# A convolution and MLP kernel on one core: first groups of 6, 8, 10 and 16 tokens, the fourth in the seven-product form, and fewer scaling steps in the last group

## The chip, the cores and the metric

The kernel runs on one core of one Trainium2 chip. The metric is device time in microseconds. The kernel before took 977.64 us (median of three runs, 976.54 to 978.36). A core has a matrix engine (PE, with weight loads shown apart as PEld), VectorE (DVE), ScalarE (ACT), GpSimd (POOL) and SyncE (SP), each with a queue of its own that it works through in program order, and 16 DMA engines.

## The reference

The input x is 8 sequences of 4224 tokens with 192 features, float32. A causal convolution of 7 taps runs along the tokens; the taps are a softmax over `weight` and each of 8 heads (24 features) has its own. On its result y follows an MLP with layer norm and a residual:

```python
mu = np.mean(x, axis=-1, keepdims=True)
var = np.mean((x - mu) ** 2, axis=-1, keepdims=True)
xn = (x - mu) / np.sqrt(var + 1e-06) * g_ln
ch = np.maximum(xn @ w_ch1, 0.0) @ w_ch2
return (x + ch).astype(np.float32)
```

Here x is y, w_ch1 is 192 x 768 and w_ch2 is 768 x 192.

## The kernel before

**Tiling.** Each of 128 partitions holds consecutive tokens; a group is n tokens on every partition. `groups` (L70) lists 18: group 0 (6 tokens), group 1 (8, the tokens left over at the ends of the sequences), group 2 (11), group 3 (15), and 14 groups of 16 (groups 4 to 17). Groups 0, 2 and 3 together are the first sequence.

**Steps of a group g.**
- `load_x` (L132) brings x with 6 tokens of halo to the tile `xg`. `first_tap` (L376, ACT or DVE) and `conv` (L408, DVE, one instruction for each tap and head) make y. In some groups `second_tap` (L393) makes the second tap on ACT and adds it to y by a DMA that accumulates (L403).
- `transpose` (L419, DVE) makes yt, with 32 features by token as PE wants it. `moments` (L431, DVE) takes statistics; `root` (L443) turns those of two groups into reciprocal standard deviations by 18 small POOL operations. The mean and g_ln are folded into w1 at the start; the reciprocal deviation is applied behind the MLP.
- `store_y` (L475) writes y to the output. The MLP's part is scaled by ACT (`scale`, L831) and added to the output in DRAM by accumulating DMAs on POOL's queue (`add_to_out`, L835). The last group is added on DVE and stored by SP.

**Up and down.** The first matmul ("up", to 768 hidden features) exists in two forms. `up` (L538) runs 144 float32 matmuls of n x 32 columns, all at L532, evicted from PSUM by ACT with the relu. `up_mixed` (L591) cuts tokens, features and two thirds of the hidden features in halves and forms seven products of sums in place of eight, with sums of w1 (`sums_of_quarters`, L562, made once) and of yt (`sums_of_y`, L575); partial results are added by accumulating DMAs (`close`, L615); the last third is plain. That is 216 matmuls, 168 of them with 256 columns and 48 with 512. The second matmul ("down") is plain in `down` (L671, 144 matmuls at L685) or in `down_fast` (L719), seven products of 36 matmuls at L738. `half_sum` and `lower_sum` (L700, L707) make its left operands on DVE, `finish_fast` (L801) its output.

Which form a group takes before the change:

| groups | up | down |
|---|---|---|
| 0, 1, 2 | plain | plain |
| 3 | plain | seven products |
| 4 to 16 (`MIXED`, L81) | seven products | seven products |
| 17 (last) | plain, 11 and 5 tokens apart | seven products on 11 tokens, plain on 5 |

**Order.** It is written out by hand: the loop at L896 and the functions issue the work of group g on PE together with DVE's, ACT's and the queues' work for groups g+1 and g+2. Inside `up_mixed(g)` stand the taps of group g+1 and the scaling of group g-1; inside `down_fast(g)` the first two taps of group g+2 between the products (`taps_behind`, L761), the transpose of g+1 and its first ten moments. Buffers of x, y and statistics exist twice, all others once; the eight PSUM banks are taken in turn, four at a time by up and one at a time by down.

Around groups 2 and 3 this order is special: iteration 2 issues both taps of group 4, the load of group 5 and the store of group 3 on POOL's queue (L914 to L918); behind `down` come `moments(3)`, `root(2)` for groups 2 and 3, and `finish(2)`, which transposes group 2's output from the copies that `park` (L812) made piece by piece. Iteration 3 stores group 4 and loads group 6 on POOL's queue (L942 to L946) and makes the sums of w1 inside `down_fast(3)` (L780). From iteration 4 on, load and store go to SP and each two iterations are alike.

Of the kernel before, what the change touches and what calls it, by code (L numbers as in the profile page):

```python
# [7 lines left out]
F32 = mybir.dt.float32  # L8
# [8 lines left out]
def kernel(  # L17
# [29 lines left out]
    nc = tc.nc  # L47
    PSUM = bass.MemoryType.PSUM
    B, S, D = x.shape
    H, K = weight.shape  # L50
    F = moe_w_ch1.shape[1]
    P = 128
# [4 lines left out]
    J = 16  # L57
    R = 2 * J
    LEFT = (S - P * R) * B // P
# [7 lines left out]

    groups = [(0, 0, 6), (None, 0, LEFT), (0, 6, J - 5), (0, J + 1, J - 1)]  # L70
    groups += [(b, j0, J) for b in range(1, B) for j0 in (0, J)]
    assert PAD <= 6 and max(n for _, _, n in groups) <= J
    NG = len(groups)
# [4 lines left out]
    NFAST = max(fast.values())  # L78
    T = C // 2

    MIXED = range(4, NG - 1)  # L81
    PAIR = NF // 2 - 1
    HJ = J // 2
    EARLY = 10
# [323 lines left out]
    def conv(g, k0=1, k1=K, heads=(0, H)):  # L408
        n = groups[g][2]
        t = xg[g]  # L410
        for k in range(k0, k1):
            for h in range(*heads):
                cs = slice(h * GRP, h * GRP + GRP)
                nc.vector.scalar_tensor_tensor(  # L414
                    out=y[g][:, 0:n, cs], in0=t[:, k : k + n, cs], scalar=taps[:, h, k : k + 1],
                    in1=y[g][:, 0:n, cs], op0=ALU.mult, op1=ALU.add,
                )
# [10 lines left out]

    sums = {}

    def moments(g, j1=0, j2=None):  # L431

        n = groups[g][2]
        if j1:
            pass
        elif g % 2:
            sums[g] = sums[g - 1][:, groups[g - 1][2] :]
        else:
            sums[g] = spool.tile([P, 2 * J, nc.vector.BN_STATS_DIM], F32, tag="st", name=f"st{g}")
        for j in range(j1, n if j2 is None else j2):  # L440
            nc.vector.bn_stats(out=sums[g][:, j, :], in_=y[g][:, j, :])  # L441

    def root(g):  # L443
        n = groups[g][2] + groups[g + 1][2]
        st = sums[g]
        dt = spool.tile([P, 2 * J], F32, tag="d", name=f"d{g}")
        vt = spool.tile([P, 2 * J], F32, tag="v", name=f"v{g}")
        rt = spool.tile([P, 2 * J], F32, tag="r", name=f"r{g}")
        d, v, r = dt[:, 0:n], vt[:, 0:n], rt[:, 0:n]

        def affine(dst, src, scale, bias):
            nc.gpsimd.tensor_scalar(
                out=dst, in0=src, scalar1=scale, scalar2=bias, op0=ALU.mult, op1=ALU.add
            )

        nc.gpsimd.tensor_tensor(d, st[:, 0:n, 1], st[:, 0:n, 4], op=ALU.subtract)
        nc.gpsimd.tensor_tensor(v, st[:, 0:n, 2], st[:, 0:n, 5], op=ALU.add)
        nc.gpsimd.tensor_tensor(d, d, d, op=ALU.mult)  # L460
        affine(v, v, 1.0 / D, 1e-6)
        affine(d, d, 0.25, 0.0)
        nc.gpsimd.tensor_tensor(v, v, d, op=ALU.add)


        affine(r.bitcast(I32), v.bitcast(I32), -0.5, float(0x5F3759DF))
        for _ in range(3):
            nc.gpsimd.tensor_tensor(d, r, r, op=ALU.mult)
            nc.gpsimd.tensor_tensor(d, d, v, op=ALU.mult)
            affine(d, d, -0.5, 1.5)  # L470
            nc.gpsimd.tensor_tensor(r, r, d, op=ALU.mult)
        rstd[g] = rt
        rstd[g + 1] = rt[:, groups[g][2] :]

    def store_y(g, queue=nc.sync):  # L475
        n = groups[g][2]
        for ps, rows in rows_of_out(g, 0, n):
            queue.dma_start(out=rows, in_=y[g][ps, 0:n].rearrange("p j d -> p (j d)"))
# [59 lines left out]
    def up(g):  # L538


        scaled = {0: (), 1: (), 2: (0, 1)}.get(g, (g - 1,))
        hidden_tile(g)
        for f in range(NF):
            for js in blocks(g):
                banks = take_set()
                rows_of_tiles(banks, yt[g][:, js], w1[:, :, f * P : f * P + P])
                evict_up(g, f, js, banks[:, :, 0 : (js.stop - js.start) * C])
            if 1 <= f <= 4:
                for s in scaled:
                    m = groups[s][2]  # L550
                    scale(s, m * (f - 1) // 4, m * f // 4)
                    if f % 2 == 0:
                        add_to_out(s, m * (f - 2) // 4, m * f // 4)

    def quarters_of_w1():
        return [
            w1[:, CH * k : CH * k + CH, P * f : P * (f + PAIR)] for k in range(2) for f in (0, FC)
        ]  # L560

    def sums_of_quarters(dst, b11, b12, b21, b22):  # L562

        for v, a, b in ((0, b12, b11), (1, b22, 0), (2, b12, b22), (3, b21, 1)):
            a, b = (dst[:, u] if isinstance(u, int) else u for u in (a, b))
            nc.vector.tensor_tensor(dst[:, v], a, b, op=ALU.subtract)
# [152 lines left out]
    def down_fast(g):  # L719
        n = fast[g]  # L720
# [37 lines left out]
                tap(g + 2, heads=(h, h + 1))  # L758
            del todo[:times]

        taps_behind = [3, 3, 3, 3, 2, 2]  # L761
        if g in MIXED:
            taps_behind = [1, 4, 4, 7, 0, 0]
        elif g + 1 in MIXED:
            taps_behind = [4, 4, 4, 4, 0, 0]
        product(0, a[:, 0, 0], b[0], c11, True)
        some_taps(taps_behind[0])
        product(1, a[:, 1, 0], w2sums[:, 2], c22, True)
# [5 lines left out]
        if g in MIXED:  # L774
            transpose(g + 1)
            moments(g + 1, 0, EARLY)
        elif g + 1 in MIXED:
            moments(g + 1)
            if g + 1 == MIXED[0]:
                sums_of_quarters(w1sums, *quarters_of_w1())  # L780
        half_sum(g, (1, 1), (1, 1), (1, 0), ALU.add)
        half_sum(g, (0, 0), (1, 1), (0, 0), ALU.add)
        half_sum(g, (0, 1), (0, 1), (1, 1), ALU.subtract)
# [47 lines left out]
    def scale(g, j1, j2):  # L831
        for j in range(j1, j2):
            nc.scalar.mul(ots[g][:, j, :], ots[g][:, j, :], rstd[g][:, j : j + 1])  # L833

    def add_to_out(g, j1, j2):  # L835
        if groups[g][0] is None:

            j1, j2 = (0, j2) if j2 == groups[g][2] else (0, 0)
        for ps, rows in rows_of_out(g, j1, j2) if j2 else ():
            nc.gpsimd.dma_start(  # L840
                out=rows, in_=ots[g][ps, j1:j2].rearrange("p j d -> p (j d)"), accum_op=ALU.add
            )
# [25 lines left out]
    def finish(g):  # L868
        ot = ots[g] if fast[g] else out_tile(g)
        left = {}  # L870
        for c, js, src in po.pop(g):
            nc.vector.transpose(  # L872
                ot[:, js, C * c : C * c + C], src.rearrange("p (j t) -> p j t", t=C)
            )
            left[js.start] = left.get(js.start, 0) + 1
            if g + 1 == NG and left[js.start] == NC - 1:
                add(g, js, slice(0, D - C))
            if g + 1 == NG and left[js.start] == NC:
                add_and_store(g, js, D - C)
# [14 lines left out]
    join_words(w2flat, *words_2)  # L894
    store_y(0)
    for g in range(NG):  # L896
        if g + 2 < NG and g not in (3, 4):
            load_x(g + 2)
        mixed, last = g in MIXED, g + 1 == NG
        if mixed:  # L900
            up_mixed(g, later)
        else:
            up(g)
        if g == 0:
            first_tap(1, False, heads=(4, H))
        if not fast[g]:

            conv(g + 1)
            transpose(g + 1)
            if g < 2:  # L910
                store_y(g + 1)
                moments(g)
            first_tap(g + 2)
            if g == 2:  # L914

                second_tap(g + 2)
                load_x(g + 3, nc.gpsimd)
                store_y(g + 1, nc.gpsimd)  # L918
            down(g)
            park(g)  # L920
            if g == 1:
                finish(0)
                root(0)
                sums_of_quarters(w2sums, *quarters_of_w2())
                moments(2)
                finish(1)
            elif g == 2:
                moments(3)
                root(2)
                finish(2)  # L930
            continue
        if not mixed:
            if not last:
                conv(g + 1, 2, 5)
            lower_sum(g)
            if not last:
                conv(g + 1, 5, K)
                transpose(g + 1)
        if g != 3 and g + 2 < NG:
            store_y(g + 1)  # L940
        parts = down_fast(g)
        if g == 3:  # L942


            store_y(g + 1, nc.gpsimd)
            load_x(g + 3, nc.gpsimd)  # L946

        if mixed:
            moments(g + 1, EARLY)
        later = sums_of_y(g + 1) if g + 1 in MIXED else iter(())  # L950
        next(later, None)
        for half in range(last, 2):
            finish_fast(g, half, *parts)
        if not last and not mixed and g + 1 not in MIXED:
            moments(g + 1)
        if not last and g % 2 == 0:
            root(g)
        if last:
            add_and_store(g, slice(0, fast[g]))
            down(g)  # L960
            finish(g)
# [30 lines left out]
```

## Time and profile before

| view | what it shows |
|---|---|
| span of the profiled run | 975.6 us (the run took 977.44) |
| busy | PE 961.7, PEld 665.4, DVE 854.3, ACT 633.9, POOL 188.5 us |
| PE clock granted | 0.999 of full speed |
| DMA | 159.63 MB, mean 164 GB/s |
| a tap of 16 tokens on DVE, L414 | 579 ns mean over all shapes, x734 |
| scaling of a token on ACT, L833 | 448 ns, x248 |
| load of a group's x on SP, 2112 KB | 15.4 us to landing (median) |
| store of a group's y on SP, 1536 KB | 10.3 us |
| add of the second tap, 768 KB | 8.2 us |
| add of `part` to `cs`, 384 KB | 10.8 us |

The page gives each engine's busy time, its share in 40 slices of the span, the chain of work that ended last (followed back from the end, at each step to what released it), groups of instructions by line, and transfers. An instruction's mean in a group of lines can mix shapes; the timeline gives one shape in one stage. "x288" after a matmul line counts records; a float32 matmul leaves two. Times from here on are microseconds from the span's start.

### The profile page before, as it was taken

What the parts mean: (1) busy time and instruction counts of PE and PEld (TensorE: products, weight loads), DVE (VectorE), ACT (ScalarE), POOL (GpSimd) and SP (SyncE); (2) the same over time, 40 slices, a digit from 0 to 9 for tenths busy, and PEclk for the clock granted to TensorE, in tenths of its full rate; (3) what the DMA queues carried; (4) which work ended last, traced back from release to release, by engine and by line L of the source; (5) the groups of instructions that cost most, each with busy time, mean ns of one, the idle gap of its engine ahead of it and who ended that gap; (6) DMA issues with size and microseconds to landing.
All of it is one profiled execution on the core that took longest, in us unless ns stands there. A gap on an engine that the chain in (4) does not pass through costs nothing.

```text
span 975.6 us, 36012 instructions
## 1 busy us (share of the span) xinstructions
PE 961.7 (99%) x16194; PEld 665.4 (68%) x16194; DVE 854.3 (88%) x1480; ACT 633.9 (65%) x1052; POOL 188.5 (19%) x334
## 2 busy tenths in 40 slices
PE   7999999999999999999999999999999999999997
PEld 5886545856758585766758576676858576685777
DVE  6999878987998989898998989899898989989407
ACT  6524637585867858595876858586785859574451
POOL 2002500113121131213221041112301141111200
PEclk9999999999999999999999999999999999999999
DMA  7233652797796969789696978869696877764141
GB/s 204 96 120 135 110 167 43 234 202 212 142 271 126 246 126 187 204 157 269 131 246 127 216 178 147 254 135 267 120 246 141 167 223 152 184 125 80 19 68 68
DMA packets 28985, 159.63 MB, mean 164 GB/s; under 512 B 3487, under 2 KB 9247, under 8 KB 21278
## 3 DMA queue, kind: packets, MB, share of 16 engines
q0 software_dynamic: 22160, 99.79, 53.0%
q1 hardware_dynamic: 6366, 57.54, 15.4%
q8 instruction: 127, 2.08, 0.8%
q14 instruction: 28, 0.23, 0.1%
q10 hardware_dynamic: 304, 0.00, 0.0%
HBM read 38.95 MB, written 50.33 MB: 92 GB/s over the span
## 4 chain that ended last, share of the span: by engine, by line
PE 95%; DVE 2%; DMA 2%; issue 0%; ACT 0%; SPq 0%
PE ps L532 48%; PE ps L738 41%; PE ps L685 5%; DMA xg<-in_x_dram 2%; DVE y L414 2%; PE ps L320 1%; DMA ga<-in_moe_g_ln_dram 0%; DVE yt L425 0%; PE ps L345 0%; DVE y L847 0%; PE ps L350 0%; PE ps L332 0%; DVE y L389 0%; ACT w L355 0%; DVE ot L872 0%
## 5 line engine op out<-in xcount | busy, mean ns | idle before, releaser
L414 DVE SCALAR_TENSOR_TENSOR y<-xg,taps,y 128x384 f32<-128x384 f32 (+4 forms) x734 | 367.9, 579 | 0.2
L532 PE MATMUL ps<-yt,w 32*128 32x256 f32 (+5 forms) x4224 | 318.7, 453 | 0.7 <-DVE yt L425 0.7
L532 PEld LDWEIGHTS ps<-yt,w 32*128 32x128 f32 x4224 | 209.0, 185 | 102.7 <-issue 84.7
L738 PE MATMUL ps<-room,w2sums 128*32 128x256 f32 (+2 forms) x4320 | 233.6, 374 | 1.0 <-issue 1.0
L738 PEld LDWEIGHTS ps<-room,w2sums 128*32 128x32 f32 x4320 | 140.7, 110 | 88.3 <-issue 1.3
L703 DVE TENSOR_TENSOR room<-room 128x1024 f32<-128x1024 f32 (+2 forms) x141 | 156.9, 1184 | 35.4 <-ACT part L744 24.9
L738 PE MATMUL ps<-room,w 128*32 128x256 f32 (+2 forms) x3240 | 179.7, 374 | 0.0
L738 PEld LDWEIGHTS ps<-room,w 128*32 128x32 f32 x3240 | 104.2, 110 | 73.5 <-ACT ot L833 9.9
L744 ACT COPY cs<-ps 128x256 f32<-128x256 f32 (+2 forms) x180 | 62.8, 364 | 100.3 <-PE ps L738 99.6
L808 DVE STREAM_TRANSPOSE ot<-cs 128x512 f32<-128x512 f32 (+2 forms) x90 | 55.7, 670 | 54.9 <-DMA cs<-part 40.6
L532 PE MATMUL ps<-ysums,w1sums 32*128 32x256 f32 x1872 | 103.3, 374 | 0.0
L613 ACT COPY room<-ps 128x2048 f32<-128x2048 f32 x39 | 72.8, 1867 | 45.3 <-PE ps L532 43.9
L532 PEld LDWEIGHTS ps<-ysums,w1sums 32*128 32x128 f32 x1872 | 95.9, 185 | 5.1
L522 ACT ACTIVATE room<-ps 128x2048 f32<-128x2048 f32 (+4 forms) x50 | 72.2, 1444 | 39.4 <-PE ps L532 39.3
L833 ACT ACTIVATE ot<-ot,r 128x192 f32<-128x192 f32 x248 | 96.7, 448 | 0.0
L840 POOL DMA_DIRECT2D out_dram<-ot x40 | 34.3, 1083 | 242.9 <-ACT ot L833 187.7
L387 ACT ACTIVATE y<-xg,taps 128x384 f32<-128x384 f32 (+4 forms) x137 | 71.7, 590 | 10.2 <-DVE st L441 8.5
L441 DVE BATCH_NORM_STATS2 st<-y 128x6 f32<-128x192 f32 x264 | 70.9, 342 | 0.0
L425 DVE STREAM_TRANSPOSE yt<-y 128x3072 f32<-128x3072 f32 (+4 forms) x19 | 56.2, 2958 | 4.8 <-PE ps L532 3.0
L685 PE MATMUL ps<-room,w 128*32 128x192 f32 (+3 forms) x1152 | 59.4, 366 | 0.0
L403 POOL DMA_DIRECT2D y<-tb x28 | 24.6, 1037 | 175.0 <-ACT cs L744 154.8
L400 ACT ACTIVATE tb<-xg,taps 128x384 f32<-128x384 f32 x112 | 58.0, 603 | 0.0
(104 smaller groups left out, 732.0 us busy)
## 6 DMA issues: line engine op xcount, KB each, us to landing
xg<-in_x_dram SPq DMA_DIRECT2D x12, 2112.0 KB, 15.4
y<-tb POOLq DMA_DIRECT2D x28, 768.0 KB, 8.2
out_dram<-ot POOLq DMA_DIRECT2D x27, 768.0 KB, 7.8
out_dram<-y SPq DMA_DIRECT2D x12, 1536.0 KB, 10.3
room<-parts_tb POOLq DMA_DIRECT2D x13, 1024.0 KB, 7.6
room<-parts_cs POOLq DMA_DIRECT2D x13, 1024.0 KB, 7.3
room<-parts_tb POOLq DMA_DIRECT2D x13, 512.0 KB, 8.6
room<-parts_cs POOLq DMA_DIRECT2D x13, 512.0 KB, 10.8
```

Of the source, the lines that this page charges most:

```text
L387: nc.scalar.mul(dst, src, tap)
L400: nc.scalar.mul(tb[g][:, 0:n, cs], xg[g][:, 1 : 1 + n, cs], taps[:, h, 1:2])
L414: nc.vector.scalar_tensor_tensor(out=y[g][:, 0:n, cs], in0=t[:, k : k + n, cs], scalar=taps[:, h, k : k + 1], in1=y[g][:, 0:n, cs], op0=AL ...
L441: nc.vector.bn_stats(out=sums[g][:, j, :], in_=y[g][:, j, :])
L522: nc.scalar.activation(dst, src, AF.Relu)
L532: nc.tensor.matmul(banks[:, q, i * w : i * w + w], right[rows, c, P * i : P * i + P], left[rows, :, c, :], start=(first and c == 0 and i = ...
L613: nc.scalar.activation(dst, src, AF.Relu) if relu else nc.scalar.copy(dst, src)
L685: nc.tensor.matmul(bank[C * q : C * q + C, 0:w], w2[:, f, C * c : C * c + C], t[:, f, q, js.start - fast[g] : js.stop - fast[g], :], start ...
L703: nc.vector.tensor_tensor(a[:, *dst, f], a[:, *left, f], a[:, *right, f], op=op)
L738: nc.tensor.matmul(dst[C * q : C * q + C, 0:w], right[:, f, C * c : C * c + C], left[:, f, q], start=(first and f == 0), stop=(f == FC - 1 ...
L744: nc.scalar.copy(to[:, c], dst[:, 0:w].rearrange("p (j t) -> p j t", t=t))
L833: nc.scalar.mul(ots[g][:, j, :], ots[g][:, j, :], rstd[g][:, j : j + 1])
```

## The change

Group 2 gets 10 tokens and group 3 gets 16 (L70), so that fifteen groups have 16. `MIXED` begins at 3: group 3 takes `up_mixed`, and the branches that served a group with plain up and seven products down go, but for the last group. Statistics are paired (3,4), (5,6) to (15,16), with groups 2 and 17 alone (`chain_of`). Iteration 2 now also makes the sums of w1 and of y for group 3, before `finish(2)` and `moments(3)`. The loads of groups 5 and 6 and the store of group 4 go to SP like all others; the store of group 3 stays on POOL's queue. In the last group the scaling of group 16 and its add to the output are done in two steps (8 tokens behind the second and the third sixth of up) in place of four steps of 4 tokens.

```diff
-    groups = [(0, 0, 6), (None, 0, LEFT), (0, 6, J - 5), (0, J + 1, J - 1)]
+    groups = [(0, 0, 6), (None, 0, LEFT), (0, 6, J - 6), (0, J, J)]
...
-    MIXED = range(4, NG - 1)
+    MIXED = range(3, NG - 1)
...
+    def chain_of(g):
+        return g - g % 2 if g < 3 else g - 1 + g % 2
...
-        n = groups[g][2] + groups[g + 1][2]
+        both = [k for k in (g, g + 1) if k < NG and chain_of(k) == g]
+        n = sum(groups[k][2] for k in both)
...
-            if 1 <= f <= 4:
+            parts = 2 if g + 1 == NG else 4
+            if 1 <= f <= parts:
                 for s in scaled:
                     m = groups[s][2]
-                    scale(s, m * (f - 1) // 4, m * f // 4)
-                    if f % 2 == 0:
-                        add_to_out(s, m * (f - 2) // 4, m * f // 4)
+                    scale(s, m * (f - 1) // parts, m * f // parts)
+                    if f % (parts // 2) == 0:
+                        add_to_out(s, m * (f - parts // 2) // parts, m * f // parts)
...
-        elif g + 1 in MIXED:
-            moments(g + 1)
-            if g + 1 == MIXED[0]:
-                sums_of_quarters(w1sums, *quarters_of_w1())
...
-        if g + 2 < NG and g not in (3, 4):
+        if g + 2 < NG:
             load_x(g + 2)
...
                 second_tap(g + 2)
-                load_x(g + 3, nc.gpsimd)
                 store_y(g + 1, nc.gpsimd)
             down(g)
             park(g)
...
                 moments(2)
+                root(2)
                 finish(1)
             elif g == 2:
+                sums_of_quarters(w1sums, *quarters_of_w1())
+                later = sums_of_y(3)
+                next(later)
+                finish(2)
                 moments(3)
-                root(2)
-                finish(2)
...
-        if g != 3 and g + 2 < NG:
+        if g + 2 < NG:
             store_y(g + 1)
         parts = down_fast(g)
-        if g == 3:
-            store_y(g + 1, nc.gpsimd)
-            load_x(g + 3, nc.gpsimd)
...
-        if not last and g % 2 == 0:
-            root(g)
+            if g % 2:
+                root(g)
+            if g + 2 == NG:
+                root(g + 1)
```

## The prediction, made before the changed kernel had run

> **What bounds the kernel now.** I read the busy shares first, then the chain that ended last, then each engine's timeline around the groups that change. The page of the kernel before says:
>
> ```profile
> PE 961.7 (99%) x16194; PEld 665.4 (68%) x16194; DVE 854.3 (88%) x1480; ACT 633.9 (65%) x1052; POOL 188.5 (19%) x334
> ...
> PE 95%; DVE 2%; DMA 2%; issue 0%; ACT 0%; SPq 0%
> ```
>
> PE is busy 99% of the span and is 95% of the chain. VectorE at 88% is the next one. The chain in order of time (start us, length us, what) shows where PE is without a gap:
>
> ```profile
> 49.80 1.79 DVE yt L425
> 51.59 0.14 issue
> 51.73 15.82 PE ps L532 x288
> 67.55 15.68 PE ps L685 x288
> 83.23 21.51 PE ps L532 x288
> 104.74 21.44 PE ps L685 x288
> 126.18 29.19 PE ps L532 x288
> 155.37 25.65 PE ps L738 x504
> 181.02 28.64 PE ps L532 x432
> 209.66 27.33 PE ps L738 x504
> ...
> 944.89 0.96 issue
> ```
>
> From 51.73 each piece begins where the last ended: group 1 (8 tokens), group 2 (11), group 3 (15), then group 4, the first with seven products in both matmuls. Until 944.89, matmul work is time and other engines matter only if PE must wait for them. Three lines of other engines decide whether it would. VectorE's timeline (start, length, engine, line, operation):
>
> ```profile
> 127.20 12.75 DVE L414 SCALAR_TENSOR_TENSOR y<-xg,taps,y 128x384 f32<-128x384 f32 x24
> ...
> 856.52 1.90 DVE L808 STREAM_TRANSPOSE ot<-cs 128x512 f32<-128x512 f32 x3 [4.22 <-DMA cs<-part]
> ...
> 881.07 3.49 DVE L712 SCALAR_TENSOR_TENSOR room<-room 128x1024 f32<-128x1024 f32 x3
> ```
>
> A tap on 16 tokens costs 12.75/24 = 0.531 us. VectorE's late half of every mixed group is anchored on a transfer (4.22 us idle until `part` was added to `cs`), and the differences of L712 end at 884.56, when PE is about to use them. ScalarE's timeline in the last group:
>
> ```profile
> 920.19 1.48 ACT L833 ACTIVATE ot<-ot,r 128x192 f32<-128x192 f32 x4
> 922.83 1.53 ACT L520 ACTIVATE room<-ps 128x352 f32<-128x352 f32 x4 [1.17 <-PE ps L532]
> 924.77 0.70 ACT L522 ACTIVATE room<-ps 128x640 f32<-128x640 f32 x1 [0.40 <-PE ps L532]
> ```
>
> Four scalings take 1.48 us, and 1.17 us is free before the next eviction.
>
> **What the Trainium skill says.** "TensorE: Matmul & The Clock Gate", section Back-to-back issue gap, gives N/2.4 + 2.5 ns for a warm matmul. The trace agrees: here a float32 matmul leaves two records, so 288 are 144 matmuls, and 15.82/144 = 109.9 ns at 256 columns (the page: 109.2), 21.51/144 = 149.4 at 352 (149.2). The same page's specification table calls the queues of ScalarE and VectorE strict FIFO, so one late operand delays all that is behind it; the 3.00 us that VectorE waited for each parked piece of group 2 (L872) with the taps of L414 queued behind agrees. "DMA: Bandwidth & Descriptors", section Issuing engines are not separate DMA queues, says that transfers of SP and GpSimd share the 16 DMA engines; so moving a load from one to the other changes when it starts, not what it competes with. The trace has no test of that.
>
> **The change, part by part.**
>
> 1. Matmuls of groups 2 and 3 (the gain). Before: 21.51 + 21.44 + 29.19 + 25.65 = 97.79 us.
>  - Group 2 keeps 144 + 144 matmuls, at 320 columns in place of 352. Up: between 109.9 (256) and 149.4 ns (352), two thirds of the way: 136.2 ns, x144 = 19.62 us. Down: between 15.68/144 = 108.9 and 21.44/144 = 148.9: 135.6 ns, x144 = 19.52 us. The skill's price, 135.8 ns, x144 = 19.56, falls between.
>  - Group 3 becomes what group 4 is: 216 matmuls up in 28.64 us, 252 down in 27.33 us. The chain repeats both figures for each mixed group. In the instruction order of the changed program this stands as said: 288 matmuls of 320 columns, then group 4's sequence once more, so a change that does nothing is no case.
>  - After: 19.62 + 19.52 + 28.64 + 27.33 = 95.11. **Gain 2.68 us.** The saving in products is mostly eaten by two facts: group 3 has a token more, and its 256-column matmuls pay the fixed 2 to 3 ns more often.
>
> 2. Does VectorE deliver group 3 in time? PE reaches it at 83.23 + 39.14 = 122.37. The taps of group 2 shrink from 264 elements to 240 (group 1's x48 took 15.88 us with 192, group 2's 19.48 with 264; so 18.3), and VectorE comes to the taps of group 3 about 84.1, held there by group 1's last parked piece (85.01 before). 48 x 0.531 = 25.5 gives 109.6; transpose 3.4: 113.0, 9 us early. The w1 sums (four of 0.95), moved here out of group 3, and three sums of y: 119.2; first wanted by the third product, 5.3 us into the group, 127.7. Then finish(2) waits for its last parked piece at 122.8, moments(3) takes 4.2 (16 x 0.26), eight taps of group 4 take 4.2, the last sum ends at 132.6. Group 4's seventh product began 196.59 - 181.02 = 15.57 in, so PE wants it at 137.9. **5.3 us to spare: cost nothing**, hidden by products 1 to 6.
>
> 3. ScalarE: the second tap of group 4 ends about 112.3 (eviction until 104.1, two times eight taps in 8.3 us, like 106.05 to 114.14 before). The parked pieces behind them are wanted only by the second PSUM set of group 3. Nothing.
>
> 4. DMAs moved. Load of group 5: from GpSimd's queue (115.67) to SP's, free when the taps of group 3 end (109.6), now ahead of the add of the second tap instead of behind it; load of group 6 and store of group 4: from GpSimd (172 us) to SP. The GpSimd queue loses the 17.54 us for which its memset waited for that load with the closings of group 4 behind it; it keeps the store of group 3 behind the tap's add, with group 3's closings behind that, first ready near 130. The add (median 8.2 us, 5.8 to 11.3) lands at 121 to 124; VectorE wants it at 127.5. If tap, load and store (1536 + 2112 + 1536 KB) all had to go through first at the best slice's 271 GB/s, that takes 19.6 us: 131.9, still before the 132.8 from which PE would wait. Nothing.
>
> 5. The rsqrt chain: pairs (3,4), (5,6) and so on in place of (4,5). It runs on GpSimd after odd groups, 18 small operations plus the memset ending some 6 us into the next group, where the first closing is ready at 7.4. One extra chain for group 2 early and one for the last group alone; neither is awaited by PE. Nothing.
>
> 6. Last group: eight scalings in each of two steps. Not shown before, so bounded. At 0.37 us each (1.48/4) they end at 923.1 and the next eviction starts 0.27 late, ends 924.6; PE wants that bank at 924.75: no loss. At the 0.448 us of the whole kernel's row they end 0.6 us later, and PE loses 0.6 twice: 1.2. The earlier adds to the output (927 and 937 before) gain nothing: the tile they free is next written at 958, where VectorE did not wait. Taken: 0.1; ends 0 and 1.2.
>
> Sum: -2.68 + 0.1 = **-2.6 us**. The profiled span of 975.6 becomes 973.0; its run took 977.44, the median of the runs is 977.64, so the prediction is 975.1. About 0.2% (1.96 us) is what a measurement of this kernel can tell from no change.
>
> **The rivals.**
> - *Mixed groups slip (slower).* L712's last difference ends at 884.56; PE's second weight block of that product is at 885.20 + 0.44 = 885.64: 1.08 us to spare. If the change makes the `part` transfer land later by d, PE loses d - 1.08 in each of 13 groups; the gain is gone at d = 1.28 and it is measurably slower from 1.43; at 1.5 the time is 977.6 - 2.6 + 13 x 0.42 = 980.5. For: all these groups swap their PSUM sets and the rsqrt's parity. Against: over twelve groups L808 starts 3.79 to 4.02 us in, whether the rsqrt comes before or not.
> - *PE waits at the head of group 3.* A tap add landing after 132.8 costs its lateness; at 134.3, 1.5 us: 976.6. Against: step 4's bound.
> - *ScalarE in the last group is slow*: step 6's upper end, 976.2.
> - *A little more:* the 0.96 us pause at 944.89, for which nothing in the profile is a cause, is gone in the new program: 974.1.
>
> **How the numbers follow.** Forecast 0.70 (975.1), slip 0.07 (980.5), head of group 3 0.07 (976.6), slow ScalarE 0.08 (976.2), pause gone 0.08 (974.1). The runs shown lie 1.1 below to 0.7 above their median. Range: 974.1 - 0.5 = 973.6 to 976.2 + 0.7 = 976.9, leaving out the slip and half of the late head. Faster by over 0.2% (under 975.7): nine tenths of the forecast (0.63) and the pause (0.08): 0.71. Slower by over 0.2%: the slip and 0.01 of a very late head: 0.08. Within: the rest, 0.21.
>
> **What would show it.** Right: in the new chain group 2's pieces are near 19.6 and 19.5, group 3's 28.64 and 27.33, group 4 starts near 178.3, and no gap stands between 51.73 and the last group. Step 2 is wrong if PE idles after 122.4 with a release by VectorE; step 4 if L414 waits there for `y<-tb`; step 6 if the up matmuls of the last group exceed 31.59 by more than 0.2; the slip if the mixed groups repeat at more than 55.97. The prediction is wrong if PE has waits that step 2 prices at nothing.

## The result and the profile after

The changed kernel takes 973.79 us (median of six runs, 973.25 to 974.69) against 978.25 us of the kernel before (six runs on the same chip, 976.54 to 978.78): ratio 0.9957, interval 0.9944 to 0.9970, that is 2.9 to 5.5 us less. Predicted were 975.1 us and a gain of 2.6; the measured time lies near the lower end of the range that was given (973.6 to 976.9). The profiled run has a span of 973.0 us. The page of the changed kernel, busy time and share of the chain:

```profile
PE 959.8 (99%) x16338; PEld 675.6 (69%) x16338; DVE 858.3 (88%) x1483; ACT 641.8 (66%) x1040; POOL 199.4 (20%) x355
...
PE 94%; DVE 2%; DMA 2%; ACT 1%; issue 0%; SPq 0%; DVEq 0%; ACTq 0%
```

PE is still nearly all of the path (94%), and it has no gap from 53.34 to the end of its work. The chain in order of time (start, length, what; lines L537, L692, L745 are L532, L685, L738 of before):

```profile
51.41 1.79 DVE yt L425
53.20 0.14 issue
53.34 15.82 PE ps L537 x288
69.16 15.68 PE ps L692 x288
84.84 19.59 PE ps L537 x288
104.43 19.52 PE ps L692 x288
123.95 28.64 PE ps L537 x432
152.59 27.33 PE ps L745 x504
179.92 28.64 PE ps L537 x432
...
907.60 31.60 PE ps L537 x546
939.20 18.93 PE ps L745 x504
958.13 8.19 PE ps L692 x240
```

Stage by stage, before to after:

| stage | before | after | difference |
|---|---|---|---|
| until PE begins group 1 | 51.73 | 53.34 | +1.61 |
| group 1 | 31.50 | 31.50 | 0 |
| groups 2 and 3 | 97.79 | 95.08 | -2.71 |
| groups 4 to 16, 13 times 55.97 | 727.68 | 727.68 | 0 |
| last group: up | 31.58 | 31.60 | +0.02 |
| last group: products of down, with the 0.96 pause before | 20.22 | 18.93 | -1.29 |
| last group: plain down and the end | 15.10 | 14.87 | -0.23 |

So the span agrees with the forecast of 973.0 partly by luck: 4.2 us were gained from group 1 on, and 1.6 of them were hidden by a start that was slower in the profiled run than in the kernel before. No edit touches the instructions of the start, and the spans of the other five runs are 0.9 to 1.5 us shorter. The lines of other engines that the prediction watched, VectorE first:

```profile
120.87 2.08 DVE L873 STREAM_TRANSPOSE ot<-parked 128x320 f32<-128x320 f32 x5
124.47 0.51 DVE L873 STREAM_TRANSPOSE ot<-parked 128x320 f32<-128x320 f32 x1 [1.52 <-ACT parked L820]
124.91 4.22 DVE L445 BATCH_NORM_STATS2 st<-y 128x6 f32<-128x192 f32 x16
129.31 4.32 DVE L414 SCALAR_TENSOR_TENSOR y<-xg,taps,y 128x384 f32<-128x384 f32 x8 [0.19 <-issue]
133.56 0.95 DVE L592 TENSOR_TENSOR ysums<-yt,ysums 128x768 f32<-128x768 f32 x1
```

The last sum of y ended at 134.5; PE's seventh product, which needs it, began at 139.52 and did not wait. The 0.19 us before the taps is where the add of the second tap had only just landed. ScalarE in the last group of the changed kernel:

```profile
919.09 2.86 ACT L834 ACTIVATE ot<-ot,r 128x192 f32<-128x192 f32 x8
921.85 1.49 ACT L525 ACTIVATE room<-ps 128x352 f32<-128x352 f32 x4
923.67 0.70 ACT L527 ACTIVATE room<-ps 128x640 f32<-128x640 f32 x1 [0.33 <-PE ps L537]
```

Eight scalings took 2.86 us; the idle time before the next eviction is used up (1.17 before), and PE lost nothing (31.60).

### The profile page after: what moved, and what is told of

It reads as the page before. It is cut to its first block, busy times and chain, and to the rows that moved or that the text cites. A ratio compares the mean times of both kernels' runs of the same rounds, so it can differ in the third digit from the quotient of the medians.

```text
span 973.0 us, 36327 instructions
## 1 busy us (share of the span) xinstructions
PE 959.8 (99%) x16338; PEld 675.6 (69%) x16338; DVE 858.3 (88%) x1483; ACT 641.8 (66%) x1040; POOL 199.4 (20%) x355
## 4 chain that ended last, share of the span: by engine, by line
PE 94%; DVE 2%; DMA 2%; ACT 1%; issue 0%; SPq 0%; DVEq 0%; ACTq 0%
PE ps L537 48%; PE ps L745 41%; PE ps L692 4%; DMA xg<-in_x_dram 2%; DVE y L414 2%; ACT w L355 0%; DMA ga<-in_moe_g_ln_dram 0%; DVE yt L425 0%; DVE y L848 0%; ACT y L387 0%; DVE spare L234 0%; DVE spare L237 0%; ACT spare L221 0%; DVE y L389 0%; DVE ot L873 0%
## 5 line engine op out<-in xcount | busy, mean ns | idle before, releaser
L414 DVE SCALAR_TENSOR_TENSOR y<-xg,taps,y 128x384 f32<-128x384 f32 (+3 forms) x734 | 367.9, 577 | 0.4 <-issue 0.2
L537 PE MATMUL ps<-yt,w 32*128 32x256 f32 (+5 forms) x4128 | 303.4, 446 | 1.0 <-DVE yt L425 0.7
L537 PEld LDWEIGHTS ps<-yt,w 32*128 32x128 f32 x4128 | 205.0, 185 | 91.6 <-issue 75.6
L745 PE MATMUL ps<-room,w2sums 128*32 128x256 f32 (+1 forms) x4320 | 233.8, 375 | 0.0
L745 PEld LDWEIGHTS ps<-room,w2sums 128*32 128x32 f32 x4320 | 140.8, 110 | 87.5
L710 DVE TENSOR_TENSOR room<-room 128x1024 f32<-128x1024 f32 (+1 forms) x138 | 154.1, 1189 | 35.4 <-ACT part L751 24.0
L745 PE MATMUL ps<-room,w 128*32 128x256 f32 (+1 forms) x3240 | 179.8, 375 | 0.0
L745 PEld LDWEIGHTS ps<-room,w 128*32 128x32 f32 x3240 | 104.1, 110 | 74.0 <-ACT ot L834 10.6
L751 ACT COPY cs<-ps 128x256 f32<-128x256 f32 (+1 forms) x180 | 63.0, 365 | 99.5 <-PE ps L745 98.8
L537 PE MATMUL ps<-ysums,w1sums 32*128 32x256 f32 x2016 | 111.3, 374 | 0.0
L537 PEld LDWEIGHTS ps<-ysums,w1sums 32*128 32x128 f32 x2016 | 103.5, 185 | 5.3
L809 DVE STREAM_TRANSPOSE ot<-cs 128x512 f32<-128x512 f32 (+1 forms) x90 | 55.9, 672 | 57.7 <-DMA cs<-part 34.2
L387 ACT ACTIVATE y<-xg,taps 128x384 f32<-128x384 f32 (+3 forms) x137 | 71.8, 590 | 11.1 <-DVE st L445 7.1
L425 DVE STREAM_TRANSPOSE yt<-y 128x3072 f32<-128x3072 f32 (+3 forms) x19 | 56.2, 2957 | 2.6 <-ACT y L324 0.8
L692 PE MATMUL ps<-room,w 128*32 128x192 f32 (+3 forms) x1152 | 57.2, 359 | 0.0
## 6 DMA issues: line engine op xcount, KB each, us to landing
xg<-in_x_dram SPq DMA_DIRECT2D x15, 2112.0 KB, 15.4
```

The source lines that it names most:

```text
L387: nc.scalar.mul(dst, src, tap)
L414: nc.vector.scalar_tensor_tensor(out=y[g][:, 0:n, cs], in0=t[:, k : k + n, cs], scalar=taps[:, h, k : k + 1], in1=y[g][:, 0:n, cs], op0=AL ...
L537: nc.tensor.matmul(banks[:, q, i * w : i * w + w], right[rows, c, P * i : P * i + P], left[rows, :, c, :], start=(first and c == 0 and i = ...
L692: nc.tensor.matmul(bank[C * q : C * q + C, 0:w], w2[:, f, C * c : C * c + C], t[:, f, q, js.start - fast[g] : js.stop - fast[g], :], start ...
L710: nc.vector.tensor_tensor(a[:, *dst, f], a[:, *left, f], a[:, *right, f], op=op)
L745: nc.tensor.matmul(dst[C * q : C * q + C, 0:w], right[:, f, C * c : C * c + C], left[:, f, q], start=(first and f == 0), stop=(f == FC - 1 ...
```

## The experiments

All are compared with the kernel before on the same chip. The chips differ: on those of the experiments the kernel before took 980.4 to 981.8 us (medians), and in the profiled runs PE began group 1 between 54.5 and 58.9. What a profile shows from group 1 on (span less start of group 1) is therefore the sharper measure, and both are given.

| run | median us | ratio to before (95%) | span from group 1 on |
|---|---|---|---|
| before, first chip | 978.25 | 1 | 923.9 |
| changed, first chip | 973.79 | 0.9957 (0.9944-0.9970) | 919.7 |
| e1 four steps | 978.56 | 0.9968 (0.9958-0.9979) | 920.3 |
| e2 two steps only | 980.81 | 0.9995 (0.9987-1.0004) | 922.8 |
| e3 sizes only | 979.87 | 0.9992 (0.9985-0.9998) | 923.4 |
| e4 two steps, late add | 978.31 | 0.9967 (0.9955-0.9980) | 919.7 |
| e5 6.2 more at the head of group 3 | 980.79 (one run) | not known | 921.6 |
| e6 12.5 more there | 990.77 (one run) | not known | 930.1 |
| e7 1.0 more in each group | 984.43 | 1.0035 (1.0024-1.0046) | 926.7 |
| e8 3.0 more in each group | 1009.5 | 1.0284 (1.0256-1.0311) | 951.3 |
| e9 load behind the add | 977.3 | 0.9969 (0.9959-0.9980) | 919.7 |
| e10 start | 978.53 | 0.9973 (0.9964-0.9981) | 920.2 |
| e11 load and start | 976.9 | 0.9967 (0.9956-0.9979) | 919.7 |
| e12 changed again | 978.29 | 0.9972 (0.9962-0.9982) | 920.1 |

**Sizes alone (e3).** The kernel before with the sizes only:

```diff
-    groups = [(0, 0, 6), (None, 0, LEFT), (0, 6, J - 5), (0, J + 1, J - 1)]
+    groups = [(0, 0, 6), (None, 0, LEFT), (0, 6, J - 6), (0, J, J)]
```

> The kernel before with groups 2 and 3 of 10 and 16 tokens, but group 3 still with a plain first matmul and the old order and queues. Theory (the seven-product form is the gain, the sizes next to nothing): group 2 at 39.1 us, group 3 at 144 x 215.8 ns = 31.1 up and 27.3 down, together 97.55 against 97.79 before: 978.0, pause as before. Rival (the gain comes from the sizes, fewer columns in the plain group): 975.6.

Its chain:

```profile
86.00 19.59 PE ps L532 x288
105.59 19.52 PE ps L685 x288
125.11 31.11 PE ps L532 x288
156.22 27.33 PE ps L738 x504
...
942.88 4.61 PE ps L738 x118
947.49 0.62 issue
```

Groups 2 and 3 take 97.55 us, as expected: the sizes give 0.24 us, and the other 2.47 of the 2.71 are the difference of 31.11 (plain) and 28.64 (seven products) in the first matmul of group 3. The pause in the last group is there again, 0.62 us.

**Two steps or four in the last group (e1, e2, e4).** e1 is the changed kernel with

```diff
-            parts = 2 if g + 1 == NG else 4
+            parts = 4
```

> The changed kernel with the last group's scaling and output adds back in four steps; all else as changed. Theory (the gain is two parts: 2.7 us of matmul work in groups 2 and 3, and the pause of PE in the last group's second matmul, which goes because the last output add no longer runs beside it): about 975.1, that is 1.3 us over the changed kernel's 973.8; the pause of near 1 us is back within 2 us of the end of the last add, and groups 2 and 3 keep 95.1 us. Rival (the pause belongs to where the instructions lie in the program, or to chance, and the two steps do nothing): 973.8, no pause. Rival (the two steps cost PE time by late evictions): under 973.8.

e2 is the kernel before with the two steps alone:

> The kernel before with only the two scaling steps in the last group. Theory (late add causes the pause): 978.25 - 1.3 = 977.0, no pause in the last group, groups 2 and 3 at 97.8 us. Rival (program layout or chance): 978.25 with the pause. If the whole gain of the change were in the two steps: 973.8.

e4 was meant to separate scaling from transfer, by issuing the adds of the changed kernel at the second and fourth sixth:

```diff
-                    if f % (parts // 2) == 0:
-                        add_to_out(s, m * (f - parts // 2) // parts, m * f // parts)
+                    if parts == 4 and f % 2 == 0:
+                        add_to_out(s, m * (f - 2) // 4, m * f // 4)
+            if g + 1 == NG and f in (2, 4):
+                for s in scaled:
+                    m = groups[s][2]
+                    add_to_out(s, m * (f - 2) // 4, m * f // 4)
```

> The changed kernel with scaling in two steps, but the two output adds issued where four steps had them. Theory (the DMA traffic of the second add beside PE's last products makes the pause): pause is back, 975.1 as with four steps. Rival (ScalarE's scaling, not the transfer, makes it): no pause, 973.8.

e4 separates nothing: GpSimd's queue holds an add only until its scaling is done, so the place in the program does not delay it, and each engine's order is that of the changed kernel. It counts as a repeat of that kernel. Beside it, e1 shows no pause and no loss in the last group (products 18.93, 978.56 against 978.31), so the theory of e1 fails: with four steps on the changed program nothing is lost. In e2 the pause is gone:

```profile
911.48 31.86 PE ps L532 x539
943.34 18.93 PE ps L739 x504
962.27 8.19 PE ps L686 x240
```

but its up is 0.27 us longer, and its median does not tell 1 us from none. The pause stood in both profiles with four steps on the old program (before, e3), each time after 118 records, and in none of the others.

The traces show what PE lacked. Instructions come by DMA too: on the page the queue q8 is of the kind "instruction", and its packets of 16 KB are one for about 255 records of PE and PEld together. The kernel before, e2 and e3 have 127 of them, the changed kernel and e1 128:

```profile
q8 instruction: 127, 2.08, 0.8%
```

In the kernel before, the 121st packet moved from 943.54 to 944.49. PE began a last record at 944.58, then stood until 945.85, 1.36 us after the packet's end. In e3 the 121st packet moved from 945.92 to 946.91; PE stopped behind 947.18 and went on at 948.11, 1.20 us after it. Measured by how far PE had come when a packet started, this one is the latest of all in both traces. The last add to the output ran just then: its packets moved from 938.96 to about 944 in the kernel before and from 941.55 to about 946.6 in e3. e2 has the same PE program, but its adds are over at 938.1; the 121st packet started at 942.64, at a record that PE of the kernel before had reached at 939.69, and ended 3.6 us before PE needed it. The changed program has 144 records of PE more in group 3, so its packets are cut at other places. In e1 one ended at 942.96, when the packets of the last add (from 942.58 on) had hardly begun, and the next, at 947.63, started with PE no further than usual. So a packet of PE's instructions that is held up by the add accounts for the pause, and either the two steps or the new program avoids it. This is read from the traces of these runs; no run was made to test it.

**Room at the head of group 3 (e5, e6).** Extra statistics on VectorE between moments(3) and the taps of group 4:

```diff
                 moments(3)
+                idle_work(3, 16)
```

with `idle_work` writing `bn_stats` of y to an unused tile; 32 in e6.

> The changed kernel with 16 extra statistics instructions on VectorE (16 x 0.26 = 4.2 us, results unused) between moments(3) and the taps of group 4. Theory (5.0 us to spare at the head of group 3: the last sum ended at 134.5, PE's seventh product begins at 139.5): group 3 still takes 28.64 up, PE does not wait, time 973.8 within noise. Rival (PE is already held by VectorE there): 4 us longer.

> The same with 32 extra instructions, 8.4 us. Theory: 8.4 - 5.0 = 3.4 us of PE idle before the seventh product of group 3, released by VectorE's last sum of y; little more behind it; time near 977. Rival (nothing of VectorE's lies on the path there): no wait.

The instructions cost more than priced, 6.28 us and 12.61 in place of 4.2 and 8.4. PE of e5:

```profile
144.66 2.87 PE L542 MATMUL ps<-ysums,w 32*128 32x256 f32 x48 [0.85 <-DVE ysums L597]
...
162.79 7.54 PE L750 MATMUL ps<-room,w2sums 128*32 128x256 f32 x136 [0.49 <-DVE room L724]
```

With 6.2 us of delay (taps from 133.15 to 139.34) PE waits 0.85 us before the seventh product, so the room there was about 5.3; a second wait follows at the differences (L724, L712 of before), and group 3 takes 1.9 us more in all. The theory's size holds for the first place, and misses the second. PE of e6:

```profile
152.44 5.50 PE L542 MATMUL ps<-ysums,w 32*128 32x256 f32 x48 [7.18 <-DVE ysums L597]
157.69 10.79 PE L542 MATMUL ps<-yt,w 32*128 32x512 f32 x96
```

With 12.5 us of delay PE is idle for 7.18: again 5.3 us of room. But the group's up grew by 10.3, because the matmuls behind the idle time ran slow: the first 48 records took 5.50 us in place of 2.77 (the last section has the clock).

**Room in every mixed group (e7, e8).** The same extra work behind `finish_fast` in groups 3 to 15 (3 and 8 instructions):

> The changed kernel with 3 extra statistics instructions (0.8 us, results unused) on VectorE in every group from 3 to 15, behind the transposes that wait for the add of part. Theory (1.1 us to spare between VectorE's differences and PE's second product of down): mixed groups still repeat every 55.97 us, time 973.8. Rival (less to spare in runs than in the profile): up to 13 x 0.8 = 10 us longer.

> The same with 8 extra instructions, 2.1 us per group. Theory: 2.1 - 1.1 = 1.0 us of PE idle in each of 13 groups, between the first and the second product of down, 13 us in all: 987. Rival (the anchor on the transfer moves with PE and takes it back): 974 to 978. Rival (the delay adds up over groups): 13 x 2.1 = 27 us longer, 1001.

VectorE of e7 and of e8, one group each:

```profile
247.87 1.11 DVE L434 BATCH_NORM_STATS2 junk<-y 128x6 f32<-128x192 f32 x3
248.90 4.30 DVE L414 SCALAR_TENSOR_TENSOR y<-xg,taps,y 128x384 f32<-128x384 f32 x8
```

```profile
310.00 3.09 DVE L434 BATCH_NORM_STATS2 junk<-y 128x6 f32<-128x192 f32 x8
313.00 4.30 DVE L414 SCALAR_TENSOR_TENSOR y<-xg,taps,y 128x384 f32<-128x384 f32 x8
```

The delays are 1.03 us (247.87 to 248.90) and 3.00 us (310.00 to 313.00). Over twelve groups, from one resumption of PE behind L724 to the same one later, the period is (894.01 - 216.09)/12 = 56.49 in e7 and (919.83 - 219.75)/12 = 58.34 in e8, against 55.97: 0.52 and 2.37 lost. So 1.03 - 0.52 = 0.51 and 3.00 - 2.37 = 0.63 us of added work cost nothing; what goes beyond is PE's delay, in each group anew.

Part of the difference to the expected 1.1 is that `part` itself landed later in these runs: counted from PE's first product on a sum of y, VectorE begins L814 on average 0.33 us (e7) and 0.22 us (e8) later than the same line, L809, in the changed kernel. The differences of L724 so end 1.38 and 3.25 us later, and the room, counted from their end, is 0.86 and 0.88 us. In e8 most of the loss is at another place than was expected, at the last sum of y:

```profile
318.32 2.87 PE L542 MATMUL ps<-ysums,w 32*128 32x256 f32 x48 [1.29 <-DVE ysums L597]
...
336.45 3.88 PE L750 MATMUL ps<-room,w2sums 128*32 128x256 f32 x68 [0.50 <-DVE room L724]
```

Over the 13 groups the first of these waits is 17.9 us and the second 6.5. Both expectations were too low, by the price of an instruction (0.34 to 0.38 us in place of 0.26) and by the room.

**The load of group 5 (e9, e12).** e9 undoes one move; e12 is the changed kernel once more on the same chip:

```diff
-        if g + 2 < NG:
+        if g + 2 < NG and g != 3:
             load_x(g + 2)
...
                 second_tap(g + 2)
+                load_x(g + 3, nc.gpsimd)
                 store_y(g + 1, nc.gpsimd)
```

> The changed kernel with one move undone: the load of group 5 is issued on GpSimd's queue behind the add of group 4's second tap, as before the change, and not on SP's queue ahead of it. Theory (the load, started 3 us earlier on another queue, shares the DMA engines with the add, and so the add lands late; behind it in one queue it would let the add through): the two halves of the first add land 7 to 10.5 us after issue in place of 11 to 15.6, ScalarE's eviction of the second product of group 3 never waits for y<-tb, group 3's up is 28.64, and the time is 0 to 0.6 us under the changed kernel's on this chip. Rival (the store of group 3 or anything else delays the add): landing as late as in the changed kernel.

> The changed kernel once more, on the same chip as the three before it. Theory: 3 to 4.3 us under the kernel before (0.9956 to 0.997).

The time from issue to landing of the first add's two halves, in the changed kernel (e12) and then in e9:

```profile
DMA to landing us min/median/max: 11.1/13.2/15.4
```

```profile
DMA to landing us min/median/max: 6.4/8.2/10.0
```

ScalarE's eviction of the second product of group 3 in e12, and what PE's fourth product waited for:

```profile
134.22 1.87 ACT L620 COPY parts_tb<-ps 128x2048 f32<-128x2048 f32 x1 [1.45 <-DMA y<-tb]
```

```profile
136.14 5.46 PE L537 MATMUL ps<-ysums,w1sums 32*128 32x256 f32 x96 [0.17 <-ACT parts_tb L620]
```

The eviction writes to the buffer `tb`, which the add still reads; so it waits for the add, the four PSUM banks that PE needs next stay full, and group 3's up takes 29.05 us (157.08 less 128.03, where the second matmul of group 2 ends). In e1 and e10 it is the same: waits of 1.65 and 1.59, up 29.25 and 29.20. In e4 the wait is 1.00 and up 28.66, so PE loses what goes beyond 1.0 us. In e9 and e11 the eviction waits for PE alone (0.71) and up is 28.64: the move is the cause. It changed two things at once, the queue and the start of the load, which e9 issues 3.7 us later (118.98 against 115.28); no run separates them. e12's own expectation is met only in part: its ratio (0.9972, from 0.9962 to 0.9982) is a gain of 1.8 to 3.7 us.

**The start (e10, e11).** `first_tap(1)` of heads 0 to 3 moves on ScalarE behind the first two evictions of group 0:

```diff
-        first_tap(1, heads=(0, 2))
...
-                first_tap(1, heads=(2, 4))
...
+            if g == 0 and f < 2:
+                first_tap(1, heads=(2 * f, 2 * f + 2))
```

> The changed kernel with the first tap of group 1's heads 0 to 3 moved on ScalarE from between the copies of w1 to behind the first two evictions of group 0's up. Theory (VectorE is the bound until group 1 and idles 0.7 to 1.2 us there for ScalarE, which is held by this step's wait for the load of group 1): PE begins group 1 about 0.8 us earlier against its own first matmul of group 0's load, time 0.8 us under the changed kernel's. Rival (the first load sets the start): no difference.

> Both edits of the two runs before. If they add: 0.8 to 1.4 us under the changed kernel's.

No gain. From the first matmul on x to group 1, e10 takes 55.37 - 18.53 = 36.84 us, and e2, with the old order and a start at the same PE clock, 54.51 - 17.67 = 36.84. ScalarE of e10 shows why:

```profile
28.42 3.16 ACT L354 COPY w<-ps 128x384 f32<-128x384 f32 x8 [1.20 <-PE ps L349]
```

its copies of w1 now wait for PE instead. They begin 9.89 us behind the first matmul on x, and 9.91 in e2 (27.58 less 17.67). e9 and e11 have the lowest medians beside the changed kernel (977.3 and 976.9 against 978.29), but the intervals overlap; that they beat it by time is not shown. For e9 the trace shows the 0.4 us.

## Why the prediction was right, point by point

- **Step 1, matmuls: right.** Forecast 95.11 us for groups 2 and 3, measured 95.08, a gain of 2.71 against 2.68; group 2 in 19.59 and 19.52 (19.62 and 19.52 forecast). e3 divides it: 0.24 for the sizes, 2.47 for the form of the first matmul. The price of the Trainium skill (TensorE: Matmul & The Clock Gate, Back-to-back issue gap) holds at a third width, 320 columns: 19.59/144 = 136.0 ns, page 135.8. The page gives it for an isolated matmul and says that it counts too much at large N in a real kernel; here it fits the spacing of a long stream of float32 matmuls, while a single record lasts 429 ns, so several are under way at once.
- **Step 2, VectorE at the head of group 3: right.** Forecast end of the last sum 132.6 with a need at 137.9; measured 134.5 and 139.52, both later by the slow start. Room 5.0 against 5.3, and e5 and e6 give 5.3. (One reading is too even: VectorE waited 3.00 us for two of the parked pieces and 1.92 for the one before.)
- **Steps 3 and 5: right.** The second tap of group 4 ended at 113.8 (112.3 forecast, and the start was 1.6 later). PE waited for GpSimd in the start alone, as before the change.
- **Step 4, the moved DMAs: right in cost on the first chip, wrong in its working.** The add was priced at its median of 8.2 us (at most 11.3). With the load ahead on SP's queue it took 11.3 to 14.4. And VectorE was taken as the one who waits, from 132.8; the eviction into `tb` waits earlier. The eviction stood 5.5 us into group 3 (129.45 less 123.95), and 0.3 us more cost nothing, so by the prediction's times PE would have lost from about 128.2 on, and the bound of 131.9 would have cost some 3.7 us (an estimate from these figures). In the changed kernel of the first chip the add landed in time, 0.19 us late for VectorE and without cost; in e1, e10 and e12 it cost 0.4 to 0.6 us. The Trainium skill (DMA: Bandwidth & Descriptors, Issuing engines are not separate DMA queues) says that transfers of different queues interleave on the same engines; e9 against e12 agrees with it. What the prediction left out is what the earlier start does to the add: with the load behind it in one queue the add landed 6.4 to 10.0 us after issue, with the load ahead in another queue 11.1 to 15.4.
- **Step 6, ScalarE in the last group: right for the changed program.** Up grew by 0.02; eight scalings took 2.86 us, under the 2.96 (twice 1.48) of the lower bound. In e2, the same steps on the old program, up grew by 0.27 in the one profile, more than the 0.2 that was named as a sign; the cause is open. (The upper bound has a slip: an eviction that ends at 925.2 for a bank wanted at 924.75 is 0.5 late, not 0.6.)
- **The pause: a rival of chance 0.08 that came true.** It was forecast as 0.96 us; the products became 1.29 shorter. This is why the measured gain is nearer 4 than 2.6. The prediction had no cause for the pause, so this part of the gain was luck. The traces give a likely one, PE's instruction packet behind the add, and by it the two steps were not needed: e1 has no pause either.
- **The slip of the mixed groups: did not happen, but its price was off.** All thirteen groups of before keep 55.97 us. The room of 1.08 us was read in one group of the kernel before. Read in the same way, the groups of the changed kernel have 0.59 to 1.56 us, 1.03 on average, and e7 and e8 give about 0.87 from the end of the differences. The rival would so have cost about 0.2 us more in each group than its working said.

## What to carry to other kernels

Where one engine is busy without a gap, its instruction count times the duration of the same shape from the same stage forecasts a change of tiling within a few hundredths of a microsecond; the uncertain part is every buffer that another engine or transfer must give back. A room read in one group is not the room of all: read it in each. For a moved transfer, list all who wait for the end of what it now runs beside, the writers of its source buffer too, and price it with the new neighbour and not with the median of a quiet stage. Where PE stands and nothing in the profile releases it, look at when the packets of its own instructions moved. When a start or a load varies from run to run, compare spans from a fixed point behind it.

## What was not expected of the hardware

PE's instructions come by DMA beside the data. Both pauses that nothing in the profile releases (0.96 us in the kernel before, 0.62 in e3) follow a packet of instructions that had started late, beside an add to the output; PE went on 1.36 and 1.20 us after the packet's end. In these two traces and e2, from the 13th packet on, PE came to the same place, 256 records on for each packet, 1.46 us or more after the packet's end, and stood for no more than its usual spacing; but for one case. In that one, in group 4 of e3, it was 1.24 us, and the group's up took 28.71 us in place of 28.64.

PE's clock after idle time. In e6 PE's work ended at 145.26 and went on at 152.44. The granted clock was 1.00 until 148.1, half of it until 158.3, and 1.00 again; the 7.18 us of idle time so cost another 3.1 us. The Trainium skill (TensorE: Matmul & The Clock Gate, Part 1: The HAM clock gate) says that an idle window of about 3.4 us sets the clock to half, and that a busy one frees it. The trace agrees in kind; here the clock fell 2.8 us after PE's work had ended and was back 5.9 us after it went on. The same fits the different starts: in e2 the first load of x let PE go on at 17.67 with the clock at 1.00, and the first fourteen records took 1.95 us; in e1 it came at 18.84, the clock stood at 0.52, and they took 3.69. The later load (1.17) and the slower records (1.74) make up the 2.90 us by which e1 begins group 1 later.
